# Attention, spectral mixing and w_ch on one core: attention ahead of the weights, x times w_ch in chunks 18 to 27, three gathers

## The chip, the cores and the metric

The kernel runs on one core of one Trainium2 chip. The core has five engines that run their own instruction queues: TensorE (PE, with its weight loads shown apart as PEld), VectorE (DVE), ScalarE (ACT), GpSimd (POOL) and SyncE (SP). POOL and SP also issue DMA transfers, which 16 DMA engines carry. The metric is device microseconds of one execution, the median of several runs; lower is better.

## What is computed

Two stages, the first feeding the second. The sizes are batch 8, heads 8, sequence 576, head width 64, model width 512 and 64 modes; all inputs and the output are float32.

```python
scores = q @ k.T / 8;  cum = cumsum(max(s, 0))
scores = where(causal, -1e9, scores + min(-(cum[:, None] - cum[None, :]), 0))
x = softmax(scores) @ v                       # [8, 576, 512] once heads are merged
X = rfft(x, axis=1)[:, :64]                   # Xr, Xi
Yr = einsum('bmd,mde->bme', Xr, w_r) - einsum('bmd,mde->bme', Xi, w_i)
Yi = einsum('bmd,mde->bme', Xr, w_i) + einsum('bmd,mde->bme', Xi, w_r)
u = x + irfft(Y padded with zeros, n=576, axis=1)
out = u + max(u @ w_ch, 0)
```

`w_r` and `w_i` are 64 matrices of 512 x 512 each, 134 MB of float32 together. Each is read once, and the DMA turns it into bf16 on the way.

## The kernel before

**Attention** (`for n in range(N)`, L583 and after). There are N = 32 iterations; iteration n is head pair g = n // 8 (128 of the 512 columns of x) and batch b = n % 8. In each, `transposes` (L348) turns q and k of the next iteration, `scores` (L382) makes 576 scores a row in two passes and ACT takes the exponential (L406, and L377 for the last 64 keys, once an iteration), `av` (L416) multiplies by v and divides into `x_all`, and `fft` (L450) takes the 64 modes of the iteration before into `xs`. There are two `xs` tiles, used by g % 2; one is cleared by a DVE memset at n = 0, the other at n = 2 (L587).

**Modes** (`modes`, L471). For each g there are eight chunks of eight modes. Chunks are counted through, 0 to 31: chunk c of group g is 8 g + c. A chunk takes two units of weights, w_r and w_i (1 MB of bf16 each, two transfers of 512 KB; the last unit in four of 256 KB), and makes 16 products of 32 columns. For g = 0 to 2 the results gather in `y_acc`; with g = 3 added they are y of that chunk. `mode_steps` (L250) says in which iteration each chunk is computed: chunks 0 to 23 within the attention, one an iteration or so from iteration 9 on, chunks 24 to 31 after it.

**Loads.** All loads of weights, q, k and v stand in one queue, POOL's, in an order written out in the program (`load`, L241). At the head of iteration n come q and k for n + 3 and n + 4 (for odd n), v for n + 3, and weights up to `on_chip[n]`. The weights go to four units inside `x_all` and `y_acc` that are not yet needed, then in turn to the rings `wpool` (5 units) and `wpool2` (3 units, given up from unit 38 on); a transfer waits until the unit that had its place has been used. `on_chip` (L256 to L271) comes from a plan that counts half units and is cut back where the rings are full; in whole units it is

```python
[3, 4, 5, 6, 7, 8, 9, 10, 12, 13, 15, 16, 18, 19, 21, 22, 24, 26, 28, 30, 32, 34, 36, 38, 40, 41, 43, 45, 45, 47, 49, 51]
```

**x times w_ch** is computed apart from y times w_ch, for 18 pairs of row blocks (`pairs`, L519). For 16 of them (`kept`) the product z is copied by ACT into a place in SBUF (`keep_product`, L536) and added later. Six (`first_pairs`) are done in the last six iterations of the attention (`first_transposed`, `first_product`); the others by `work()` (L737), which turns the rows of a pair (`x_transposed`, L656) and keeps the pair before (`keep`, L681). `TAKE` says how many calls follow each chunk of the last group.

**The last group.** y of each chunk is turned (`y_transposed`, L693). For chunks 0 to 3 of the group `gather_round` (L713) brings y and v = y times w_ch together into `yv`, where the rows of all modes stand below each other, 64 rows at once. For chunks 4 and 5 y is gathered so too, but v is computed by `y_times_wch` (L701) and goes to `yv` by a DMA of 128 KB on SP (`spread`, L512). Chunks 6 and 7 are spread both ways. While weights of chunk 6 are awaited, PE computes z of the last kept pair, and between the products of chunk 7 the z sums of pairs 0 and 1 (`first_z`) and the u of pair 0 (`first_u`).

**The end** is a list of steps (L961 and after) that sums, takes the maximum and writes out the 18 pairs, by PE, ACT, DVE, POOL and SP. A DMA of two elements (`mark`, L884) on SP, ahead of the spreads of chunk 6, waits for the last weights.

Of the kernel before, what the change touches and what calls it, by code (L numbers as in the profile page):

```python
# [10 lines left out]
FP32 = mybir.dt.float32  # L11
FP16 = mybir.dt.float16
BF16 = mybir.dt.bfloat16
# [6 lines left out]
def kernel(  # L20
# [11 lines left out]
    nc = tc.nc  # L32
    B, H, S, D = q.shape
    NM = moe_w_r.shape[0]
    DM = H * D
# [68 lines left out]

    xs = [gp.tile([P, 2, 2, 2, 2, B, HM], BF16, name=f"xs{i}") for i in range(2)]
    xs_flat = [t.rearrange("p q k h r b m -> p (q k h r b m)") for t in xs]
# [103 lines left out]
    def ring_of(k):  # L210
        if k < NE:
            return None
        return int(k < LW2 and (k - NE) % (WA + WB) >= WA)
# [35 lines left out]
    NW = 2  # L249
    mode_steps = {B: [0, 1, 2, 3], B + 1: [4], B + 2: [5], B + 4: [6], B + 6: [7]}  # L250
    for c in range(NCK, (NG - 1) * NCK):
        mode_steps.setdefault(B + c - (0 < c % NCK < 4), []).append(c)
    used = [NW * sum(len(cs) for t, cs in mode_steps.items() if t < n) for n in range(N + 1)]
    W0 = 2
    on_chip = []
    for n in range(N):  # L256
        w = 4 + 2 * (WA + WB + NE - 2) * (n + 1) // (B + 1) if n < B else plan + (3 if n <= 2 * B else 4)
        plan = w

        nt, ring = 0, ([], [])  # L260
        while nt < min(w // 2, len(wq)):
            i = ring_of(nt)
            if i is not None:
                depth = (WA, WB)[i]
                if len(ring[i]) >= depth and ring[i][-depth] >= used[n]:
                    break
                ring[i].append(nt)
            nt += 1
        if nt < w // 2:
            plan = 2 * nt + 1  # L270
        on_chip.append(2 * nt)  # L271

# [178 lines left out]
    def fft(n):  # L451
        if n < 0:
            return
        g, b = divmod(n, B)
        ps = auxpool.tile([P, 2, 3 * HM], FP32, name="ft_ps", tag="aux")
        for T in range(NT):
            nT = tails[T]
            for q_ in range(2):
                nc.tensor.matmul(  # L459
                    ps[HP * q_ : HP * q_ + HP].rearrange("p h f -> p (h f)"),  # L460
                    x_all[:nT, g, b, T, q_::2], Ff_sb[:nT, T, :],
                    start=(T == 0), stop=(T == NT - 1),
                    tile_position=(0, HP * q_), skip_group_check=True,
                )
        for h in range(2):
            for q_ in range(2):
                a = ps[HP * q_ : HP * q_ + HP, h, : 2 * HM].rearrange("p (r m) -> p r m", r=2)
                a = bass.AP(tensor=a.tensor, offset=a.offset, ap=[a.ap[0], [HM, 2]] + list(a.ap[1:]))
                nc.vector.tensor_copy(out=xs[g % 2][HP * h : HP * h + HP, q_, :, h, :, b, :], in_=a)  # L469

    def modes(g, c, meanwhile=None):  # L471


        ps = auxpool.tile([P, DM], FP32, name="yp", tag="aux")
        cols = xs[g % 2].rearrange("p q k h r b m -> p q k (h r b) m")

# [50 lines left out]

    first_pairs = [i for i in kept[1:] if pairs[i][0][1] < NF and pairs[i][0][0] <= 4][:6]
    z1s, xts1 = {}, {}

    def kept_place(i, t):

        z1s[i] = t.bitcast(FP32).rearrange("p (x e) -> p x e", x=2)

    def keep_product(i, xx, z):
        nc.scalar.copy(out=z1s[i][:, xx], in_=z)  # L536

    def first_transposed(i, x):
        b, T = pairs[i][x]
        ps = auxpool.tile([P, DT, P], FP32, name="xt_ps", tag="aux")  # L540
        for dt in range(DT):
            nc.tensor.matmul(
                ps[:, dt, :], x_all[:, dt, b, T, :], ident16h, start=True, stop=True,
                skip_group_check=True,
            )
        xts1[i, x] = spool.tile([P, DT, P], FP16, name="xt1", tag="yt")
        nc.vector.tensor_copy(out=xts1[i, x], in_=ps)

    open_unit = {}

    def half_of(pool, name):
# [6 lines left out]
        return t[:, :HU]  # L558

    def first_product(i, x):  # L560
        if x == 0:
            kept_place(i, half_of(wpool2, "z1"))
        ps = auxpool.tile([P, DM], FP32, name="z1_ps", tag="aux")
        for dt in range(DT):
            nc.tensor.matmul(  # L565
                ps, xts1[i, x][:, dt, :], wch_sb[:, dt, :], start=(dt == 0), stop=(dt == DT - 1)
            )
        keep_product(i, x, ps)


# [5 lines left out]
    with tc.tile_pool(name="sc_psum", bufs=2, space=PSUM) as scpool, \  # L576
# [8 lines left out]
        for n in range(N):  # L585
            if n in (0, 2):
                nc.vector.memset(xs_flat[n // 2].bitcast(FP32), 0.0)  # L587
# [18 lines left out]
            scores(n, 1)  # L606
            i = first_pairs[n - N + len(first_pairs)] if n >= N - len(first_pairs) else None
            if i is not None:
                first_transposed(i, 0)
            transposes(n + 1, 1)  # L610
            fft(n - 1)
            av(n, 0)
            if i is not None:
                first_product(i, 0)
                first_transposed(i, 1)
            if i is not None:
                first_product(i, 1)
        av(N - 1, 1)
# [17 lines left out]

    NLOC = 5
    old = xs_flat[0]
    xt_sb = [
# [4 lines left out]

    places = [finpool.tile([P, 4 * DM], BF16, name="r_sb", tag="r", bufs=3) for i in range(2)]
    places += [finpool.tile([P, 4 * DM], BF16, name=f"z1_{i}") for i in range(NLOC)]
    places.append(old[:, 4 * DM : 8 * DM])
    places += [y_acc[:, c : c + 2, :].rearrange("p c e -> p (c e)").bitcast(BF16) for c in (0, 2)]
# [31 lines left out]

    def keep(i):  # L681
        x_times_wch(i, True)
        j = late.index(i)
        kept_place(i, places[j])
        for x in range(2):
            keep_product(i, x, zs.pop((i, x)))
# [25 lines left out]

    def gather_round(c0, c1, b0, which, pool):  # L713

        n = 2 * MC * (c1 - c0)
        ng = P // n
        ps = pool.tile([P, DM], FP32, name="g_ps", tag="u" if pool is upool else "aux")
        for dt in range(DT):
            op = yt_first[:, dt, c0 % NY : c0 % NY + c1 - c0].rearrange("p c (x b) -> p (c x) b", b=B)
            for g in range(ng):  # L720
                nc.tensor.matmul(
                    ps[n * g : n * g + n, :] if which else ps[n * g : n * g + n, bass.ts(dt, P)],
                    op[:, :, b0 + g],
                    wch_sb[:, dt, :] if which else ident16h,
                    start=(dt == 0 or not which), stop=(dt == DT - 1 or not which),
                    tile_position=(0, n * g), skip_group_check=True,
                )

        def copies(engine=None):
            copy = {"v": nc.vector.tensor_copy, "s": nc.scalar.copy}[engine or ("s" if which else "v")]  # L730
            for g in range(ng):
                copy(out=yv[2 * MC * c0 : 2 * MC * c1, b0 + g, which, :], in_=ps[n * g : n * g + n, :])

        return copies

# [13 lines left out]

    late = [i for i in kept if i not in first_pairs]  # L750
    order_z = late[:-1]
    TAKE = (3, 2, 3, 0, 0, 0)
    us, rs = {}, {}
# [89 lines left out]
    def z_of(i):  # L843
        return [zs[i, x] for x in range(2)]

    for c in range(NCK - 2):
        yb = modes(NG - 1, c)
        for x in range(TAKE[c] - 1):
            work()
        if c == NCK - 3:  # L850
            x_transposed(late[-1])
            x_transposed(0)
        yt = y_transposed(yb, c)
        if TAKE[c]:
            work()
        if c >= NY:
            if c == NCK - 3:
                x_times_wch(0, False)
                x_transposed(1)
            y_times_wch(c, yt)  # L860
            if c == NCK - 3:
                for x in range(2):
                    gather_round(NY, NCK - 2, 4 * x, 0, upool)("sv"[x])
        elif c == NY - 1:
            for x, pool in enumerate((auxpool, upool, auxpool, auxpool)):
                for which in (1, 0):
                    gather_round(0, NY, 2 * x, which, pool)()
                if x >= 2:
                    work()
    assert not order_z and not ahead  # L870
    c = NCK - 2
    yb6 = modes(NG - 1, c, {2: lambda: keep(late[-1])})
    x_times_wch(1, False, (0,))
    yt = y_transposed(yb6)
    x_times_wch(1, False, (1,))
    vb6 = y_times_wch(c, yt)


# [11 lines left out]
    def first_z(i):  # L890
        add_y(z_of(i), i, 1, slice(0, GK))
        add_last(z_of(i), i, vb6, c=0)

    yb = modes(NG - 1, NCK - 1, {2: lambda: (first_z(0), first_z(1)), 3: first_u})

# [90 lines left out]
```

## Time and profile before

| what | us |
|---|---|
| median of 3 runs (438.44 to 439.22) | 439.2 |
| the profiled execution, its own time | 440.17 |
| its span, first to last instruction | 438.4 |
| PE busy | 339.6 (77%) |
| DVE busy | 251.8 (57%) |
| ACT busy | 227.6 (52%) |
| POOL busy | 172.5 (39%) |

The span is what the rows of the trace cover; the profiled execution took 1.8 us more than that. The loads through POOL's queue are 81.3 MB as written, the transfers of SP's queue 11.1 MB, of which the output is 9.4. Times in rows of the trace are microseconds from the first instruction. In a row such as `393.23 0.67 PE L479 MATMUL yp<-w_sb,xs ... x8 [1.32 <-DMA w_sb]` stand the start, the length, the engine, the line of the program, the operation with what it writes and reads, how many instructions were drawn together, and in brackets how long the engine had been idle and what ended that. A table by stretch gives for each engine the busy time and, in brackets, the number of instructions, then the granted clock of TensorE (1.00 is full), the mean busy share of the 16 DMA engines (it may pass 1, as packets overlap) and what they wrote in GB/s. The attention's last exponential of a 64-key block starts at 325.16 us, chunk 31's last products at 404.90 us, and the last output is issued at about 435 us.

### The profile page before, as it was taken

Reading aid. Unit: us, or ns where it says so; the run is one execution under the profiler, and the core shown is the slowest. Engines: PE = TensorE matmul, PEld = TensorE weight load, DVE = VectorE, ACT = ScalarE, POOL = GpSimd, SP = SyncE. Lnnn points to the kernel's source line nnn. Section 1 sums busy time; section 2 is a strip of 40 time slices with the busy share of each in tenths; the row PEclk is TensorE's granted clock in tenths of the full one; section 3 lists DMA queues with packets and bytes.
Section 4 is the critical chain, followed back from the end, with each engine's and each line's share of the span. In section 5 each row is a group of like instructions: output and inputs, shape, how many; then the busy total and the mean of one; then the engine's idle time right before and its main releaser. Section 6 shows DMA issues by size and latency. Waiting matters only on the chain. (4 is left out here: it accounts for less than half of the span.)

```text
span 438.4 us, 10539 instructions
## 1 busy us (share of the span) xinstructions
PE 339.6 (77%) x4362; PEld 204.0 (47%) x4409; DVE 251.8 (57%) x572; ACT 227.6 (52%) x424; POOL 172.5 (39%) x258
## 2 busy tenths in 40 slices
PE   1687989899695967973938447888887977778995
PEld 1455666466463544651615224655653535332441
DVE  7667776577564545662624415666655444370796
ACT  1487788268463625760726124666660434330795
POOL 6556354434354444323443433333322221310493
PEclk9999999899987969995877858999997998998999
DMA  9999999999999999999999999999999999996598
GB/s 167 207 207 205 206 206 207 207 209 208 207 205 207 209 207 210 208 209 209 204 209 208 210 208 209 207 210 206 212 211 212 211 211 212 211 216 122 186 380 340
DMA packets 68409, 93.09 MB, mean 212 GB/s; under 512 B 25278, under 2 KB 27066, under 8 KB 68362
## 3 DMA queue, kind: packets, MB, share of 16 engines
q0 software_dynamic: 61424, 81.28, 105.0%
q1 hardware_dynamic: 6938, 11.14, 7.0%
q8 instruction: 34, 0.56, 0.5%
q14 instruction: 13, 0.11, 0.1%
HBM read 163.37 MB, written 9.51 MB: 394 GB/s over the span
## 5 line engine op out<-in xcount | busy, mean ns | idle before, releaser
L406 ACT ACTIVATE p_sb<-sc_ps,cumt_sb 128x576 f16<-128x576 f32 (+1 forms) x256 | 141.7, 636 | 21.8 <-PE sc_ps L398 21.4
L245 POOL DMA_DIRECT2D v<-in_v_dram x72 | 51.3, 713 | 62.1 <-DMA w_sb<-in_moe_w_i_dram 13.5
L398 PE MATMUL sc_ps<-qt,kt 128*128 128x320 bf16 (+2 forms) x337 | 65.6, 299 | 11.3 <-ACT kt L360 6.5
L245 POOL DMA_DIRECT2D w_sb<-in_moe_w_i_dram x62 | 38.4, 620 | 89.2 <-PE yp L479 29.3
L360 DVE COPY qt<-tr_ps 64x576 bf16<-64x576 bf16 x64 | 47.8, 746 | 39.9 <-PE tr_ps L356 39.9
L479 PE MATMUL yp<-w_sb,xs 128*32 128x512 bf16 (+1 forms) x480 | 43.3, 439 | 30.1 <-DMA w_sb<-in_moe_w_i_dram 26.7
L356 PE MATMUL tr_ps<-ident,qk 64*64 64x64 bf16 x1152 | 34.9, 206 | 30.9 <-DMA qk<-in_k_dram 14.6
L245 POOL DMA_DIRECT2D w_sb<-in_moe_w_r_dram x60 | 37.3, 622 | 54.0 <-DMA w_sb<-in_moe_w_r_dram 33.3
L398 PEld LDWEIGHTS <-kt 128*128 128x128 bf16 x384 | 38.4, 105 | 36.1 <-ACT kt L360 14.1
L392 PE MATMUL sc_ps<-negm,ident 128*128 128x256 bf16 x256 | 54.0, 296 | 0.0
L356 PEld LDWEIGHTS <-qk 64*64 64x64 bf16 x1152 | 26.9, 119 | 48.9 <-DVE kt L360 18.9
L377 ACT ACTIVATE p<-sc_ps,cumt 128x64 f16<-128x64 f32 x32 | 10.0, 313 | 74.0 <-PE sc_ps L373 74.0
L434 PE MATMUL av_ps<-v,p_sb 128*128 128x65 f16 x1024 | 44.1, 197 | 1.8 <-DVE x_all L444 0.7
L360 ACT COPY kt<-tr_ps 64x576 bf16<-64x576 bf16 x32 | 22.8, 714 | 40.6 <-DVE qt L360 40.0
L434 PEld LDWEIGHTS <-p_sb 128*128 128x128 f16 x1024 | 37.5, 99 | 9.4 <-DVE x_all L444 5.5
L469 DVE CAST xs<-ft_ps 64x128 bf16<-64x128 f32 x128 | 36.7, 287 | 7.0 <-PE ft_ps L459 5.6
L479 PEld LDWEIGHTS <-xs 128*32 128x32 bf16 (+1 forms) x512 | 17.5, 146 | 48.2 <-DMA w_sb<-in_moe_w_i_dram 26.4
L439 DVE TENSOR_REDUCE den<-av_ps 128x5 f32<-128x10 f32 x64 | 10.9, 170 | 49.7 <-PE av_ps L434 48.8
L444 DVE TENSOR_TENSOR x_all<-av_ps,rcp 128x320 f16<-128x320 f32 x64 | 31.5, 492 | 2.2
L499 DVE TENSOR_TENSOR y_acc<-yp,y_acc 128x512 f32<-128x512 f32 x16 | 11.1, 692 | 28.9 <-PE yp L479 28.2
L459 PE MATMUL ft_ps<-Ff_sb,x_all 128*64 128x192 f16 (+1 forms) x320 | 24.2, 264 | 1.0 <-DVE x_all L444 1.0
L536 ACT COPY z<-z_ps 128x512 f32<-128x512 f32 x22 | 12.9, 585 | 22.8 <-PE z_ps L565 14.2
(112 smaller groups left out, 444.8 us busy)
## 6 DMA issues: line engine op xcount, KB each, us to landing
w_sb<-in_moe_w_r_dram POOLq DMA_DIRECT2D x60, 512.0 KB, 13.5
w_sb<-in_moe_w_i_dram POOLq DMA_DIRECT2D x55, 512.0 KB, 13.2
out_dram<-r_w SPq DMA_DIRECT2D x16, 512.0 KB
v<-in_v_dram POOLq DMA_DIRECT2D x72, 64.0 KB, 11.2
qk<-in_q_dram POOLq DMA_DIRECT2D x15, 288.0 KB, 12.0
qk<-in_k_dram POOLq DMA_DIRECT2D x15, 288.0 KB, 13.2
x_all<-in_moe_w_r_dram POOLq DMA_DIRECT2D x4, 512.0 KB, 9.0
w_sb<-in_moe_w_i_dram POOLq DMA_DIRECT2D x3, 384.0 KB, 12.7
```

What stands on the lines that cost most here:

```text
L245: nc.gpsimd.dma_start(out=dst, in_=src)
L356: nc.tensor.transpose(ps[rows, r, :], src[rows, r, :], ident16[rows, rows])
L360: copy(out=to[:, :, :, half * RH : half * RH + RH], in_=ps[HP * i : HP * i + HP].rearrange("d r (h p) -> d h p r", h=2),)
L392: nc.tensor.matmul(ps[:, bass.ds(w * S, W)], ident16, negm[:, bass.ts(r, W)], start=True, stop=False, skip_group_check=True,)
L398: nc.tensor.matmul(ps[:, c0 : c0 + i1 - i0], keys[:, w, r, :], qh[:, i0:i1], start=False, stop=True, skip_group_check=True,)
L406: nc.scalar.activation(out=pt[:, poff[x] : poff[x] + S - w * W], in_=ps[:, w * S : (w + 1) * S - w * W], func=ACTF.Exp, bias=cumt_sb[:, x, ...
L434: nc.tensor.matmul(ps[:, I, r : r + NCH], lhsT, rhs, start=(i == 0), stop=(i == len(todo) - 1), skip_group_check=True,)
L444: nc.vector.tensor_tensor(out=x_all[:, g, b, :, D * h : D * h + D], in0=ps[:, :, 1 : NCH], in1=rcp.unsqueeze(2).to_broadcast([P, NT, D]), ...
L459: nc.tensor.matmul(ps[HP * q_ : HP * q_ + HP].rearrange("p h f -> p (h f)"), x_all[:nT, g, b, T, q_::2], Ff_sb[:nT, T, :], start=(T == 0), ...
L469: nc.vector.tensor_copy(out=xs[g % 2][HP * h : HP * h + HP, q_, :, h, :, b, :], in_=a)
L479: nc.tensor.matmul(ps[32 * cg : 32 * cg + 32, :], cols[k0:, q_, 1 - ri, :, c * MC // 2 + cg], wt[(g, c, ri)][cg // 2][k0:, 2 * (cg % 2) + ...
L536: nc.scalar.copy(out=z1s[i][:, xx], in_=z)
```

## The change

Five edits that belong together. The order of weights is written as a formula, one unit per iteration and another every eight, and 15 chunks are left to the time after the attention: `mode_steps` now holds chunks 0 to 16. Since chunks 17 to 23 of group 2 then run while group 3's modes are being written, there is a third `xs`, cleared at n = 4. The products x times w_ch leave the attention: `first_pairs`, `first_transposed` and `first_product` go, and `work()` is called after chunks 18 to 27 by a new `TAKE`; the places of the kept products change with that. `gather` replaces `gather_round`: y and v of chunks 0 and 1, 2 and 3, 4 and 5 of the last group are gathered, 32 rows each time, so v of chunks 4 and 5 no longer goes by DMA. In chunk 6, z of the last kept pair and of pairs 0 and 1 moves behind the products, and `first_z(0)` ahead of chunk 7's.

```diff
-    xs = [... for i in range(2)]
+    xs = [... for i in range(3)]
+    XS = (0, 1, 2, 0)
...
-    mode_steps = {B: [0, 1, 2, 3], B + 1: [4], B + 2: [5], B + 4: [6], B + 6: [7]}
-    for c in range(NCK, (NG - 1) * NCK):
-        mode_steps.setdefault(B + c - (0 < c % NCK < 4), []).append(c)
+    mode_steps = {
+        B: [0, 1, 2, 3], 9: [4], 10: [5], 12: [6], 14: [7], 16: [8], 18: [9], 19: [10], 21: [11], 23: [12],
+        25: [13], 26: [14], 28: [15], 30: [16],
+    }
+    done = [c for t in sorted(mode_steps) for c in mode_steps[t]]
...
     for n in range(N):
-        w = 4 + 2 * (WA + WB + NE - 2) * (n + 1) // (B + 1) if n < B else plan + (3 if n <= 2 * B else 4)
...
-        on_chip.append(2 * nt)
+        w = 3 + n if n < B else 4 + n + (n - B) // B
...
+        on_chip.append(2 * w)
...
-            if n in (0, 2):
+            if n in (0, 2, 4):
                 nc.vector.memset(xs_flat[n // 2].bitcast(FP32), 0.0)
...
-            i = first_pairs[n - N + len(first_pairs)] if n >= N - len(first_pairs) else None
-            if i is not None:
-                first_transposed(i, 0)
             transposes(n + 1, 1)
             fft(n - 1)
             av(n, 0)
-            if i is not None:
-                first_product(i, 0)
-                first_transposed(i, 1)
-            if i is not None:
-                first_product(i, 1)
...
-    NLOC = 5
-    old = xs_flat[0]
+    NLOC = 3
+    old = xs_flat[1]
...
+    places = [lambda: half_of(wpool2, "z1")] * (2 * WB)
+    places.append(old[:, 4 * DM : 8 * DM])
...
+    places += [xs_flat[2][:, i * 4 * DM : (i + 1) * 4 * DM] for i in range(2)]
...
+    def gather(c0, c1, turns, kinds, then=None):
+        n = 2 * MC * (c1 - c0)
+        rows = slice(2 * MC * c0, 2 * MC * c1)
+        ng = P // n
+        for b0 in range(0, B, ng):
+            for which in kinds:
+                pool, tag = then if then and b0 else (auxpool, "aux")
+                ps = pool.tile([P, DM], FP32, name="g_ps", tag=tag)
+                for dt in range(DT):
+                    for g in range(ng):
+                        op = yt_first[:, dt, c0 % NY : c0 % NY + c1 - c0].rearrange("p c (x b) -> p (c x) b", b=B)
+                        nc.tensor.matmul(
...
+                            tile_position=(0, n * g), skip_group_check=True,
+                        )
+                for g in range(ng):
+                    dst, src = yv[rows, b0 + g, which, :], ps[n * g : n * g + n, :]
+                    if (which == 0 and (b0 == 0 or g < 2)) if then else g % 2:
+                        nc.vector.tensor_copy(out=dst, in_=src)
+                    else:
+                        nc.scalar.copy(out=dst, in_=src)
...
-    late = [i for i in kept if i not in first_pairs]
+    late = list(kept)
...
-    TAKE = (3, 2, 3, 0, 0, 0)
+    TAKE = {18: 2, 19: 2, 20: 2, 21: 2, 22: 2, 23: 2, 24: 1, 25: 1, 26: 1, 27: 1}
...
+    for c in range(len(done), (NG - 1) * NCK):
+        modes(c // NCK, c % NCK)
+        for x in range(TAKE.get(c, 0)):
+            work()
     for c in range(NCK - 2):
         yb = modes(NG - 1, c)
-        for x in range(TAKE[c] - 1):
-            work()
         if c == NCK - 3:
             x_transposed(late[-1])
             x_transposed(0)
         yt = y_transposed(yb, c)
-        if TAKE[c]:
+        for x in range(TAKE.get((NG - 1) * NCK + c, 0)):
             work()
-        if c >= NY:
-            if c == NCK - 3:
-                x_times_wch(0, False)
-                x_transposed(1)
-            y_times_wch(c, yt)
-            if c == NCK - 3:
-                for x in range(2):
-                    gather_round(NY, NCK - 2, 4 * x, 0, upool)("sv"[x])
...
+        if c == NCK - 3:
+            x_transposed(1)
+        if c % 2:
+            gather(c - 1, c + 1, (), (1, 0), (upool, "u"))
...
-    yb6 = modes(NG - 1, c, {2: lambda: keep(late[-1])})
-    x_times_wch(1, False, (0,))
+    yb6 = modes(NG - 1, c)
+    keep(late[-1], (0,))
     yt = y_transposed(yb6)
-    x_times_wch(1, False, (1,))
+    keep(late[-1], (1,))
     vb6 = y_times_wch(c, yt)
+    x_times_wch(0, False)
+    x_times_wch(1, False)
...
-    yb = modes(NG - 1, NCK - 1, {2: lambda: (first_z(0), first_z(1)), 3: first_u})
+    first_z(0)
+    yb = modes(NG - 1, NCK - 1, {2: lambda: first_z(1), 3: first_u})
```

## The prediction

> **What bounds the kernel now.** I read first the forty slices of the page, then the sums by stretch, then who waits for whom, then the rows in order of time. In the slices, three rows matter: TensorE's clock, the share of the DMA engines and the bytes they write.
>
> ```profile
> PE   1687989899695967973938447888887977778995
> PEclk9999999899987969995877858999997998998999
> DMA  9999999999999999999999999999999999996598
> GB/s 167 207 207 205 206 206 207 207 209 208 207 205 207 209 207 210 208 209 209 204 209 208 210 208 209 207 210 206 212 211 212 211 211 212 211 216 122 186 380 340
> ```
>
> The DMA row stands at 9 from the first slice to the thirty-sixth, about 395 us, while PE drops to 1, 3 and 4 tenths on the way. So the stream of loads is the bound up to about 404 us. By stretch (busy time of PE, PEld, DVE, ACT, POOL; then granted clock, DMA share, GB/s):
>
> ```profile
> 22.00:77.00 55.00, 48.25 (x793) 32.86 (x798) 39.91 (x106) 43.33 (x82) 28.15 (x44) 1.00 1.21 206
> 77.00:264.00 187.00, 137.22 (x1988) 85.89 (x2016) 95.67 (x234) 88.80 (x165) 74.39 (x115) 0.83 1.18 208
> 330.00:398.00 68.00, 54.36 (x486) 28.69 (x484) 32.85 (x55) 22.95 (x40) 14.59 (x24) 0.92 1.12 212
> 414.00:437.00 23.00, 19.36 (x90) 7.72 (x87) 18.92 (x18) 19.55 (x39) 16.45 (x14) 1.00 0.99 384
> ```
>
> The share is above 1.1 in every stretch of loading, and the rate moves only with the mix: 206 GB/s where one weight unit comes per iteration, 212 where there are weights alone. After 409 us the end is a chain of sums with ACT full and the output written at 384 GB/s. The waits say the same:
>
> ```profile
> ACT p L377 <- PE sc_ps L373: 74.0, 31, 11.6
> POOL w_sb L245 <- DMA w_sb<-in_moe_w_r_dram: 47.1, 28, 3.1
> POOL w_sb L245 <- DMA w_sb<-in_moe_w_i_dram: 31.2, 24, 2.0
> POOL w_sb L245 <- PE yp L479: 30.4, 7, 7.0
> ```
>
> POOL, which issues all loads, is held mostly by earlier loads that have not landed. The attention (ACT's 74 us at L377) pays for it, at no cost to the end. Last, the stretch in which the last two chunks of weights land:
>
> ```profile
> 393.23 0.67 PE L479 MATMUL yp<-w_sb,xs 128*32 128x512 bf16 x8 [1.32 <-DMA w_sb<-in_moe_w_i_dram]
> ...
> 398.73 0.67 PE L479 MATMUL yp<-w_sb,xs 128*32 128x512 bf16 x8 [1.91 <-DMA w_sb<-in_moe_w_r_dram]
> 399.33 0.12 PEld L764 LDWEIGHTS <-G_sb 96*128 96x128 f16 x2 [0.38 <-issue]
> ...
> 402.92 0.65 PE L479 MATMUL yp<-w_sb,xs 128*32 128x512 bf16 x4
> ...
> 403.62 0.26 SPq L884 DMA_DIRECT2D mark<-w_sb  x1
> ...
> 404.90 0.65 PE L479 MATMUL yp<-w_sb,xs 128*32 128x512 bf16 x4
> ```
>
> SP's mark at 403.62 waits for the last weights alone, so they land at 403.6. The last products start at 404.90, 1.3 us later: from 399.3 on PE, not the load, sets the end, because the sums of z for pairs 0 and 1 (399.33 to 402.92) ran at half clock:
>
> ```profile
> 395.98:399.39 3.41, 1.50 (x13) 0.51 (x12) 0.69 (x1) 0.00 (x0) 0.00 (x0) 1.00 0.97 181
> 399.39:402.80 3.41, 3.41 (x14) 0.90 (x12) 0.00 (x0) 0.00 (x0) 0.00 (x0) 0.50 0.53 99
> ```
>
> PE was busy 1.50 of 3.41 us in the first of these stretches, and in the next the granted clock is 0.50.
>
> **The change, part by part.** *Order of the loads.* The bytes stay the same; units of weights move behind the attention. Through iteration 9 both plans give 3, 4, 5 and so on to 10, 12, 13 units. Then the old plan adds one and a half to two units per iteration, the new one a single unit and an extra one every eight. What this costs hangs on whether the DMA engines ever run dry. Two iterations then load 2 units (2.10 MB) and attention data (two tiles of 288 KB, four of 64 KB: 0.85 MB); 2.95 MB at 206 GB/s are 14.3 us, 7.2 each, and the extra unit (1.05 MB at 212, 4.95 us) over eight iterations makes 7.8. PE needs 6.6 us for an iteration that waits for nothing (L373 at 96.71 and 103.13 are 6.4 apart; L377 at 60.83 and 67.56 are 6.7 apart) and 1.09 us for a chunk (L479, sixteen products). Thirteen chunks in iterations 9 to 31 add 0.6: 7.2 us. So the loads stay slower than PE by about half a microsecond an iteration, and POOL starts iteration 9 with loads that take 12 to 14 us from issue to landing queued ahead. I take 0 us; the attention ends near 262 us instead of 330 (73.7 us, 16 for iteration 8, 22 of 7.8). The bound on the other side is the third rival's: 3.5 us.
>
> *Third xs and its clearing.* One more DVE memset of 1.76 us (L587) at iteration 4. At iteration 2 the same memset made that iteration 7.7 us instead of 6.6, so 1.1 us of PE, covered by the queue of loads (9 to 11 us to landing there). 0 us; 1.1 if that queue were empty.
>
> *Products x times w_ch.* The six pairs done in the last six iterations go (L542 4.6, L565 12.4 us of PE; iterations of 9.3 and 10.4 us there) and come back among chunks 18 to 27. One call costs PE 0.62 + 1.9 us, DVE 1.4, ACT 1.2; two per chunk are 5 us, with the chunk 6.1, under 9.9 us for a chunk's two units at 212 GB/s. Even all at half clock, 12 us now and then is covered by three units in flight, 14.8 us. 0 us.
>
> *Three gathers.* Each makes 2 rounds of v (16 products, 1.1 us each) and y (16, 0.36), then 16 copies, 10 on ACT (0.58) and 6 on DVE (0.69). Those of chunks 1 and 3 of the last group lie in 9.9 us of load each: 0. For the one of chunk 5, ACT has 5.8 us of copies from about 387.3, done near 393.1, a hair before chunk six's copies need ACT (394). I charge 0.4 us, since chunk 5 now starts from an idle PE, thus at half clock; bounds 0 and 1.3.
>
> *Two spreads of v less.* The SP transfers of v for chunks 4 and 5 go: 128 KB each, at 212 GB/s 0.62 us of the stream each. The first comes before chunk six's last weights, the second before chunk seven's: chunk six lands 0.6 earlier, the end of weights 1.2. Bounds: 0 (if the engines had room) and 1.0 for chunk six, by nothing better than that load rates at 384 to 388 us show 220 against 212 GB/s in sum.
>
> *The path from chunk six to the last product of chunk seven.* Before: 393.23 to 405.55, 12.3 us, with 1.9 idle and about 1.7 lost to the clock. After, at full clock: products 0.6; keep's first half 0.87; ACT copies z and then yt, 0.59 and 0.58, so v starts at 2.95 (the transposes and keep's second half, 0.40 and 0.87, lie inside); v 0.87; sums of pairs 0 and 1 that were done in earlier waits, 16 matmuls of 0.216, 3.46; first z of pair 0 four of them, 0.86; products 0.5; z of pair 1 half of 1.79, 0.9; products 0.5; first u 1.40 (403.50 to 404.90); products 0.65. Sum 12.1. So 3.8 us of PE work moved behind chunk six is paid by the filled 1.9 us and by the clock. What is queued behind the moved z on ACT is yt alone, and v waits for it; that is in the sum.
>
> *The end.* From 405.55 on nothing changes: 32.9 us of span.
>
> **Sum.** 0.6 earlier landing, 0.2 shorter path, 0.4 later ACT: 0.4 to 0.5 us less. The profiled execution took 440.2 us, 1.8 around its span of 438.4, so it would take 439.7; it stands 1.0 above the median 439.2, which becomes 438.7 us.
>
> **Rivals.** *Clean path:* ACT is done in time and the spread's whole effect is felt: 0.2 + 1.0, 438.0 us. For: DVE and ACT sums above; against: PE idles before chunk five. The Trainium skill, "TensorE: Matmul & The Clock Gate", section "HAM oscillation — how this bites in real kernels", asks for no PE gaps over about 3.4 us; by that rule the waits of about 2 us around chunk six cost no clock and this case stands, while here a gap of 1.9 us was enough, so I do not follow it.
>
> *The clock falls inside the path.* The gather of chunk 5 ends on PE near 389, its next work is 0.6 us, and chunk six lands near 392.5. A stretch like 395.98 to 399.39 then falls before the path and the next 3.41 us run at half clock: up to 1.7 us, 1.3 where ACT's copies are waited for anyway. 0.5 less and 1.3 to 1.7 more: 440.0 us at most, 439.9 taken.
>
> *The loads run dry* (the other side). POOL issues q of iteration n+3 only when PE has transposed iteration n. The queue of some 10 us lasts 22 iterations if PE takes 0.45 us more than the loads, so it decides from 7.8 + 0.45 = 8.25 us an iteration; what PE takes beyond that is lost to the stream for good. At 8.4 us it is 22 times 0.15, some 3.5 us with the start of an empty queue: 442.7. For: mean clock 0.83 from 77 to 264 us, and each half-clock stretch costs 1.7 us. Against: these lie behind waits that now go; from 22 to 77 us the clock is 1.00.
>
> *It does not do what it says:* loads still lead, attention waits as before, 439.2.
>
> **How the numbers follow.** A measurement tells about 0.2% here, 0.9 us. Forecast 0.36 (0.13 faster by more than that, 0.20 within, 0.03 slower), clean path 0.22 (0.20 and 0.02), clock 0.16 (0.09 within, 0.07 slower), dry 0.19 (slower), no effect 0.07 (within). Faster 0.33, same 0.38, slower 0.29. The range, 437.2 to 442.0, leaves out about 0.04 below and 0.11 above; the forecast's own is 438.0 to 439.4.
>
> **What would show it.** Right: the last L373 near 258 us; DMA row at 9 until the same slice; no yv<-v_sb spread before the mark; the mark near 402.4; last products of chunk seven near 405.0 and the same 33 us after. Wrong: a slice under 9 between 90 and 262 us with POOL waiting for PE tr_ps (dry); clock 0.50 between 392 and 404 (clock); a copy of yt over 0.5 us late behind L732 copies on ACT (gather); a tail longer than 33 us would be something I have not priced.

## The result, and the profile after

The changed kernel is slower by half a per cent: 441.7 us median of 11 runs (440.58 to 442.78) against 439.2 of 11 runs of the kernel before on the same chip; the ratio is 1.0047, 95% interval 1.0031 to 1.0063, so about 2.1 us more by the ratio, where 438.7 us was forecast. Its profiled execution took 441.87 us with a span of 440.1; before it was 440.17 with 438.4. The two traces can be compared for the 1.7 us between their spans. They do not stand alike in their runs: the execution of before is 1.0 us above its median, the one of after 0.2.

The slices of the page after, the rows that were read before:

```profile
PE   1598889899999799699699995577776758289995
PEclk9998999999999799999699999888888686679999
DMA  9999999999999999999999999999999999995498
GB/s 166 207 206 206 204 207 207 208 208 207 204 206 208 207 208 210 199 206 209 208 208 208 195 212 211 212 211 211 211 211 211 211 211 211 211 211 109 167 382 335
```

The DMA row stays at 9 to the same slice, so the loads do not run dry for long. But PE's weak slices have moved: it is mostly at 8 and 9 to slice 24, and in the twelve after it at 5 to 8 but for one at 2; the clock is .6 to .8 in slices 26 to 36, up to the end of the loads. In the row of rates two slices stand out, 199 GB/s from 176 to 187 us and 195 from 242 to 253. The same stretches as before (busy time of PE, PEld, DVE, ACT, POOL; clock, DMA share, GB/s):

```profile
22.00:77.00 55.00, 48.72 (x792) 33.21 (x790) 39.95 (x100) 41.92 (x79) 28.54 (x44) 0.97 1.21 206
77.00:264.00 187.00, 166.02 (x2646) 107.56 (x2645) 125.98 (x317) 123.17 (x232) 81.02 (x126) 0.95 1.19 206
330.00:398.00 68.00, 43.55 (x441) 21.84 (x440) 24.81 (x37) 27.96 (x49) 14.56 (x24) 0.75 1.12 211
414.00:437.00 23.00, 20.90 (x97) 8.41 (x94) 20.30 (x19) 21.09 (x42) 17.71 (x15) 1.00 0.93 361
```

From 77 to 264 us PE now works 166 instead of 137 us, at clock 0.95 instead of 0.83, and the stream writes 206 instead of 208 GB/s: the attention runs ahead. Its last L371 (L377 before) starts at 263.9 instead of 325.2 us. From 330 to 398 us the clock is 0.75. The waits:

```profile
POOL w_sb L246 <- DMA w_sb<-in_moe_w_i_dram: 54.2, 33, 2.6
POOL w_sb L246 <- DMA w_sb<-in_moe_w_r_dram: 49.1, 31, 2.2
...
ACT p L371 <- PE sc_ps L367: 35.6, 30, 5.6
...
POOL w_sb L246 <- PE yp L473: 17.6, 6, 5.3
```

ACT's wait for scores, 74.0 us before, is halved. That is off the path. What sets the end is the stretch from chunk six on, in order of time (start, length, engine, line):

```profile
390.57 5.87 ACT L703 CAST yv<-g_ps 32x512 f16<-32x512 f32 x10 [2.01 <-PE g_ps L691]
...
390.80 4.19 DVE L701 CAST yv<-g_ps 32x512 f16<-32x512 f32 x6 [1.05 <-PE g_ps L691]
...
392.95 1.22 PE L473 MATMUL yp<-w_sb,xs 128*32 128x512 bf16 x16 [1.09 <-ACT yv L703]
...
395.02 0.69 DVE L497 TENSOR_TENSOR y_sb<-yp,y_acc 128x512 f16<-128x512 f32 x1
...
395.77 0.40 PE L662 MATMUL yt_ps<-ident16h,y_sb 128*128 128x128 f16 x4 [0.62 <-DVE y_sb L497]
...
396.46 0.59 ACT L529 COPY y_acc<-z_ps 128x512 f32<-128x512 f32 x1
396.95 0.59 ACT L664 COPY yt_sb<-yt_ps 128x512 f16<-128x512 f16 x1
...
397.59 1.04 PE L670 MATMUL v_ps<-wch_sb,yt_sb 128*128 128x512 f16 x4 [0.57 <-ACT yt_sb L664]
...
398.47 1.89 PE L641 MATMUL z_ps<-wch_sb,xs 128*128 128x512 f16 x8
...
400.19 1.89 PE L641 MATMUL z_ps<-wch_sb,xt_x 128*128 128x512 f16 x8
...
402.88 0.67 PE L473 MATMUL yp<-w_sb,xs 128*32 128x512 bf16 x8
...
403.51 0.26 SPq L851 DMA_DIRECT2D mark<-w_sb  x1
...
406.44 0.65 PE L473 MATMUL yp<-w_sb,xs 128*32 128x512 bf16 x4
```

The same rows of the kernel before:

```profile
393.95 0.69 DVE L503 TENSOR_TENSOR y_sb<-yp,y_acc 128x512 f16<-128x512 f32 x1 [1.42 <-PE yp L479]
...
395.14 0.58 ACT L698 COPY yt_sb<-yt_ps 128x512 f16<-128x512 f16 x1 [2.28 <-PE yt_ps L696]
```

Four things are to be seen. The copies of the gather keep DVE to 394.99 and ACT to 396.44, so y of chunk six is summed at 395.02 (before 393.95) and turned y copied at 396.95 (before 395.14). PE waits twice for them, 0.62 and 0.57 us. Only behind v come the sixteen products of z for pairs 0 and 1 (398.47 to 402.1), which nothing had held back. And chunk seven's first products start at 402.88, although their weights landed at 398.48. The last products end at 407.09, 1.54 us later than before, and the end after them takes 33.0 us of span as before (32.85).

In the records of the loads, each with one execution (us from the span's start; "last" is the last quarter of chunk seven; the last column is the time from the issue of the last output to the end of the span):

| kernel | chunk 5 landed | chunk 6 | last | last products end | behind the last issue |
|---|---|---|---|---|---|
| before | 382.24 | 393.19 | 403.60 | 405.55 | 3.06 |
| after | 383.76 | 393.48 | 403.50 | 407.09 | 3.19 |
| a_both_old | 383.51 | 393.63 | 405.27 | 407.11 | 3.72 |
| b_new_tail | 382.29 | 392.90 | 402.80 | 405.82 | 5.00 |
| c_gather_old | 382.92 | 393.22 | 403.61 | 406.83 | 3.74 |
| d_z_old | 383.75 | 393.69 | 403.64 | 407.40 | 3.20 |
| f_z0_first | 382.15 | 393.81 | 404.22 | 404.92 | 3.06 |
| h_old_tail_z0 | 383.49 | 393.68 | 404.04 | 404.73 | 3.74 |
| c_warm | 383.69 | 394.00 | 404.43 | 407.24 | 4.07 |
| g_unit_early | 383.08 | 393.02 | 403.01 | 406.61 | 3.19 |
| i_fill | 382.76 | 392.71 | 403.31 | 404.79 | 3.19 |
| m_fill_unit | 382.90 | 392.84 | 403.72 | 405.02 | 3.18 |
| k_spread_off | 382.36 | 393.34 | 403.38 | 406.62 | 4.47 |
| l_spread_thrice | 383.05 | 394.29 | 405.50 | 415.12 | 3.35 |

From chunk six's landing to the end of the last products, which is called the path below, it is 12.36 us before and 13.61 after: 1.25 of the 1.7 us. The rest is 0.29 of landing and 0.1 of the end. The last column will matter below: from the issue of the last output on no engine computes, and yet it is not the same in all kernels. The traces of a_both_old, c_gather_old and d_z_old are 2.2, 1.0 and 1.3 us above the medians of their kernels, so single rows of these say little of the usual execution.

### The profile page after: what moved, and what is told of

Its sections match the earlier page's. It is cut to its first block, busy times and chain, and to the rows that moved or that the text cites. A ratio compares the mean times of both kernels' runs of the same rounds, so it can differ in the third digit from the quotient of the medians.

```text
span 440.1 us, 10802 instructions
## 1 busy us (share of the span) xinstructions
PE 349.0 (79%) x4497; PEld 205.6 (47%) x4497; DVE 255.9 (58%) x577; ACT 237.9 (54%) x442; POOL 172.4 (39%) x258
## 3 DMA queue, kind: packets, MB, share of 16 engines
q1 hardware_dynamic: 6650, 10.88, 6.8%
## 5 line engine op out<-in xcount | busy, mean ns | idle before, releaser
L392 PE MATMUL sc_ps<-qt,kt 128*128 128x512 bf16 (+2 forms) x384 | 75.4, 308 | 6.7 <-ACT kt L354 5.5
L473 PE MATMUL yp<-w_sb,xs 128*32 128x512 bf16 (+1 forms) x480 | 41.8, 425 | 36.9 <-DMA w_sb<-in_moe_w_i_dram 31.1
L392 PEld LDWEIGHTS <-kt 128*128 128x128 bf16 x384 | 37.0, 103 | 35.1 <-ACT kt L354 14.5
L386 PE MATMUL sc_ps<-negm,ident 128*128 128x256 bf16 x256 | 53.0, 291 | 0.2
L350 PE MATMUL tr_ps<-ident,qk 64*64 64x64 bf16 x1152 | 31.9, 200 | 21.6 <-DVE kt L354 19.3
L350 PEld LDWEIGHTS <-qk 64*64 64x64 bf16 x1152 | 24.6, 113 | 35.2 <-DVE kt L354 25.8
L529 ACT COPY z<-z_ps 128x512 f32<-128x512 f32 x18 | 10.5, 585 | 46.0 <-PE z_ps L641 33.8
L641 PE MATMUL z_ps<-wch_sb,xs 128*128 128x512 f16 x96 | 30.7, 476 | 0.0
L371 ACT ACTIVATE p<-sc_ps,cumt 128x64 f16<-128x64 f32 x32 | 10.0, 313 | 35.6 <-PE sc_ps L367 35.6
```

The source lines that it names most:

```text
L350: nc.tensor.transpose(ps[rows, r, :], src[rows, r, :], ident16[rows, rows])
L386: nc.tensor.matmul(ps[:, bass.ds(w * S, W)], ident16, negm[:, bass.ts(r, W)], start=True, stop=False, skip_group_check=True,)
L392: nc.tensor.matmul(ps[:, c0 : c0 + i1 - i0], keys[:, w, r, :], qh[:, i0:i1], start=False, stop=True, skip_group_check=True,)
L473: nc.tensor.matmul(ps[32 * cg : 32 * cg + 32, :], cols[k0:, q_, 1 - ri, :, c * MC // 2 + cg], wt[(g, c, ri)][cg // 2][k0:, 2 * (cg % 2) + ...
L641: nc.tensor.matmul(zs[i, x], xts[i][:, x, dt, :], wch_sb[:, dt, :], start=(dt == 0), stop=(last and dt == DT - 1), skip_group_check=True,)
```

## The experiments

Ratios are to runs of the kernel before on the same chip (medians there 439.6 us, 21 to 25 runs).

**Which part costs: one back at a time.** Four kernels: `a_both_old` is the changed kernel with both late parts (gather of chunks four and five, places of z) as before, so its order of loads, with the third xs, the products x times w_ch and the gathers of chunks one and three in their new form; `c_gather_old` has the old gather, `d_z_old` the old places of z; `b_new_tail` is the kernel before with both new late parts.

```diff
 # a_both_old and c_gather_old, against after: chunks 4 and 5 (gather_round is put back)
-        if c % 2:
-            gather(c - 1, c + 1, (), (1, 0), (upool, "u"))
+        if c >= NY:
+            ...
+            y_times_wch(c, yt)
+            if c == NCK - 3:
+                for x in range(2):
+                    gather_round(NY, NCK - 2, 4 * x, 0, upool)("sv"[x])
+        elif c % 2:
+            gather(c - 1, c + 1, (), (1, 0), (upool, "u"))
 # a_both_old and d_z_old, against after: z of pair 0 in chunk 5, then chunks 6 and 7
         if c == NCK - 3:
+            x_times_wch(0, False)
             x_transposed(1)
...
-    yb6 = modes(NG - 1, c)
-    keep(late[-1], (0,))
+    yb6 = modes(NG - 1, c, {2: lambda: keep(late[-1])})
+    x_times_wch(1, False, (0,))
     yt = y_transposed(yb6)
-    keep(late[-1], (1,))
+    x_times_wch(1, False, (1,))
     vb6 = y_times_wch(c, yt)
-    x_times_wch(0, False)
-    x_times_wch(1, False)
...
-    first_z(0)
-    yb = modes(NG - 1, NCK - 1, {2: lambda: first_z(1), 3: first_u})
+    yb = modes(NG - 1, NCK - 1, {2: lambda: (first_z(0), first_z(1)), 3: first_u})
```

> The changed kernel's attention, order of weights and products among chunks 18 to 27, but chunks 4 to 7 of the last group as before: gather of 4 and 5 with v by DMA, and z of pairs 17, 0 and 1 in their old places. Theory (the loss of 2 us is made in those last chunks): last products of chunk seven near 405.5 us, time at the kernel before's, within 0.5 us. Rival (the new order of loads loses time in the stream): weights land 0.6 us or more later than 403.6, time 0.6 to 2 us above before.

> The changed kernel, with chunks 4 and 5 gathered as before (y alone on PE, v by DMA), z of pairs 17, 0 and 1 in the new places. Theory of the gather (its 10 copies on ACT and 6 on DVE hold up y and yt of chunk six by about 1.2 us): 1.0 to 1.5 us below the changed kernel. Rival (the 16 moved matmuls alone lengthen PE's path): less than 0.4 us below it.

> The changed kernel with its three gathers, but z of pairs 17, 0 and 1 and the first z in their old places. Theory of the gather: yt of chunk six still late, and the old half-clock stretch may come back: within 0.7 us of the changed kernel. Rival (the moved matmuls): 1.3 us or more below it, at before's time.

> The kernel before with chunks 4 to 7 of the last group in their new form (gather of 4 and 5 with v on PE, z behind chunk six, first z of pair 0 ahead of chunk seven), all else as before. Theory (last chunks): 1.5 to 2.5 us above before, as in the changed kernel; yt of chunk six copied over a microsecond later than 395.14 because copies of yv are ahead of it. Rival (order of loads): at before's time or up to 1 us below, since two DMA transfers of v go.

| kernel | median us | ratio | interval |
|---|---|---|---|
| a_both_old | 440.34 | 1.0019 | 1.0006 to 1.0032 |
| c_gather_old | 441.25 | 1.0046 | 1.0027 to 1.0065 |
| d_z_old | 440.80 | 1.0027 | 1.0016 to 1.0039 |
| b_new_tail | 442.71 | 1.0072 | 1.0057 to 1.0086 |

a_both_old is 0.8 us above before, and I had put all that is new in it at nothing. But this is not yet a price of the order of loads: in its trace 0.7 us more than before (3.72 against 3.06) lie behind the issue of the last output, where no weights are awaited. The new places of z cost 0.9 to 1.2 us (after against d, c against a; in both pairs the ends behind the last issue are alike, but the intervals overlap a little). The new gather costs nothing that can be told beside the new places of z (after against c) and 0.4 us without them (d against a; the intervals overlap); in both pairs the kernel with the old gather ends about 0.5 us longer behind the last issue, so equal times do not show that the gather is free. That the path of c gains nothing has a reason in its trace, three stretches around the landing of its chunk six at 393.22:

```profile
389.00:393.00 4.00, 1.84 (x42) 0.85 (x41) 3.15 (x5) 2.30 (x4) 0.17 (x1) 0.93 1.12 211
393.00:396.40 3.40, 3.13 (x17) 1.23 (x17) 0.99 (x2) 0.20 (x1) 0.00 (x0) 0.51 1.12 223
396.40:400.00 3.60, 3.60 (x19) 1.53 (x18) 0.69 (x1) 1.46 (x3) 0.00 (x0) 1.00 1.08 203
```

The row of PE that starts that path:

```profile
393.26 1.08 PE L473 MATMUL yp<-w_sb,xs 128*32 128x512 bf16 x8 [2.43 <-DMA w_sb<-in_moe_w_i_dram]
```

Without the new gather's products PE is busy for 1.84 of 4 us and waits 2.43 us for the landing, and the clock falls to 0.51 in the path itself: turned y is copied 3.46 us after the landing, as in after (3.47). So in that execution the rival in which the clock falls happened, in this kernel though not in after. Of b_new_tail's 3.1 us, 1.9 lie behind the last issue (see k_spread_off); its turned y is copied at 395.67, 0.5 us later than before, where the theory had over a microsecond.

**The short path before, the order of loads again, PE kept busy, one unit earlier.** `f_z0_first` puts the first z sum of pair 0 ahead of chunk seven and changes nothing else; `h_old_tail_z0` does the same to a_both_old. `c_warm` is c_gather_old with ten products more in the wait of chunk six, into a place that is then started anew. `g_unit_early` is after with one unit more in the plan from iteration 26 on.

```diff
 # f_z0_first, against before
-    yb = modes(NG - 1, NCK - 1, {2: lambda: (first_z(0), first_z(1)), 3: first_u})
+    first_z(0)
+    yb = modes(NG - 1, NCK - 1, {2: lambda: first_z(1), 3: first_u})
 # c_warm, against c_gather_old
-    yb6 = modes(NG - 1, c)
+    yb6 = modes(NG - 1, c, {2: busy})
 # g_unit_early, against after
         w = 3 + n if n < B else 4 + n + (n - B) // B
+        w += n >= 26
```

> The kernel before with one edit: the z sums of pair 0 stand ahead of chunk seven's products and not between them. Theory (from chunk six on the end is set by PE, and the half-clock stretch from 399.4 us comes from the idle 1.9 us before it): the idle time is filled, no half clock there, last products at 404.3 us behind the last weights at 403.6 and not at 405.55; 1.0 to 1.4 us below before. Rival (the end hangs on the weights alone): within 0.4 us of before.

> The changed kernel's attention and order of loads with the old last chunks (as in a_both_old) and that same single edit. Theory: 0.5 to 1.4 us below a_both_old, so about at before's time; above f_z0_first by what the order of loads costs, 0.5 to 1.0 us. Rival (the order of loads costs nothing, a_both_old was 0.8 above by chance): equal to f_z0_first within 0.4 us.

> c_gather_old with ten idle matmuls in the wait for chunk six's last weights, into a bank of z that is overwritten by the next product; nothing else. Theory (without the gather PE idles, the clock falls to 0.50 at 393 us and takes back what the gather's absence gives): the clock stays at 1.00 from 392 to 404, last products about 12.3 us after chunk six's landing and not 13.6; 0.8 to 1.4 us below c_gather_old. Rival (the moved matmuls themselves are the 1.2 us): within 0.4 us of c_gather_old.

> The changed kernel with one unit of weights more from iteration 26 on. Theory (the rate falls to 146 to 185 GB/s at 246 to 249 us because few bytes are in flight behind small loads of v): the dip goes or shrinks, weights land 0.4 to 0.7 us earlier, 0.3 to 0.7 us below the changed kernel. Rival (the dip costs nothing, or is not of the order): no difference over 0.3 us.

f_z0_first: 439.31 us, 0.9998 (0.9985 to 1.0011); the gain that was expected of it is not there, though its trace has no half clock in the path and its last products start with the landing:

```profile
404.24 0.25 SPq L884 DMA_DIRECT2D mark<-w_sb  x1
...
404.27 0.65 PE L479 MATMUL yp<-w_sb,xs 128*32 128x512 bf16 x4 [0.39 <-DMA w_sb<-in_moe_w_i_dram]
```

There its end is set by the loads, so a shorter path can give no more. That the kernel before loses time to the path in its profiled execution (1.3 us behind the landing) and yet gains nothing here suggests that this execution, 1.0 us above the median, is not the usual one. h_old_tail_z0: 440.25 us, 1.0014 (1.0005 to 1.0023), 0.9 us above f_z0_first on the same chip, as was expected. Yet its trace does not show the cause that was expected: its weights land 0.2 us earlier than those of f_z0_first and its last products end 0.2 us earlier, and again 0.7 us (3.74 against 3.06) lie behind the last issue. c_warm: 442.43 us, 1.0051 (1.0037 to 1.0065), by the ratios 0.2 us above c_gather_old: the gain that the theory expected is not there. The clock was at 1.00 from 393.0 us on, through the whole path. But the ten products, from 392.40 on, held chunk six's last products to 394.93, 0.9 us behind the landing (0.04 in c_gather_old). The path is 13.24 us against 13.61, so most of what the clock gives is taken back by the delay; what a clock kept up without delay would give is not shown. g_unit_early: 441.35 us, 1.0037 (1.0025 to 1.0050), 0.4 us under after, with intervals that overlap. In its slice from 242 us the rate is 204 GB/s and not 195, but i_fill, without the unit, has 202 there.

**Same instructions, other order in chunk six; and the spreads.** `i_fill` is after with five lines reordered: z of pair 0 stands before the turning of y, the copy of turned y ahead of the copies of z on ACT. `m_fill_unit` adds g_unit_early's line. `k_spread_off` is f_z0_first with the new gather in place of the two v spreads; `l_spread_thrice` is the kernel before with each of them sent three times.

```diff
 # i_fill, against after
-    keep(late[-1], (0,))
+    x_times_wch(0, False)
     yt = y_transposed(yb6)
-    keep(late[-1], (1,))
+    keep(late[-1])
     vb6 = y_times_wch(c, yt)
-    x_times_wch(0, False)
     x_times_wch(1, False)
 # k_spread_off, against f_z0_first
-            y_times_wch(c, yt)
-            if c == NCK - 3:
-                for x in range(2):
-                    gather_round(NY, NCK - 2, 4 * x, 0, upool)("sv"[x])
+                gather(NY, NCK - 2, (), (1, 0), (upool, "u"))
 # l_spread_thrice, against before
-            spread(c, 1, vb)
+            for _ in range(3):
+                spread(c, 1, vb)
```

> The changed kernel, same instructions, other order on PE and ACT in chunk six: the z sums of pair 0 before the turning of y, the copy of yt on ACT ahead of the two copies of z, both halves of the kept product before v. Theory (the moved sums cost because they stand behind v, while PE waits for yt): PE is busy from 394.2 on without a wait, chunk seven's first products start near 401.5 instead of 402.9, last products near 405.8, 1.3 us less, 440.4 us, ratio 1.0015 to 1.0025. Rival (the work itself is too much for the time there is, or the landing sets the end): 0 to 0.3 us less, 1.0040 to 1.0047.

> The same order, and one unit of weights more in the plan from iteration 26 on, so that the weights land 0.4 us earlier. If path and stream both limit in part: 0.3 to 0.5 us less than i_fill, 440.0 us, ratio 1.0008 to 1.0018. If the path alone sets the end: the same as i_fill.

> The kernel before with the new gather of v for chunks four and five, so the two transfers of v gone, and the first z sum of pair 0 ahead of chunk seven; z of the other pairs in its old places. Theory (the spreads cost the weights 0.3 to 0.8 us, and with the short path the end follows the landing): 0.3 to 0.8 us less than the kernel before, 438.8 to 439.3, ratio 0.9982 to 0.9993. Rival (the gather's copies on ACT make yt of chunk six late and take it all back): 439.6 to 440.3, ratio 1.0000 to 1.0016.

> The kernel before, with the two transfers of v for chunks four and five sent three times each, so 512 KB more on SP's queue. Theory (they take their time from the weights, 0.62 us each): last weights 2 to 2.5 us later, 441.6 us, ratio 1.0045 to 1.0055; so two fewer would give 1.2 us of landing. Rival (the engines have room for them): 439.3, ratio within 1.0010.

i_fill: 439.82 us, 1.0009 (1.0000 to 1.0019), 1.7 us under after by the two ratios: the theory's side, even below its range. Its path, in order of time:

```profile
392.17 1.24 PE L473 MATMUL yp<-w_sb,xs 128*32 128x512 bf16 x16 [1.01 <-ACT yv L703]
...
393.34 1.90 PE L641 MATMUL z_ps<-wch_sb,xs 128*128 128x512 f16 x8
...
394.31 0.69 DVE L497 TENSOR_TENSOR y_sb<-yp,y_acc 128x512 f16<-128x512 f32 x1
...
395.07 0.39 PE L662 MATMUL yt_ps<-ident16h,y_sb 128*128 128x128 f16 x4
...
395.67 0.58 ACT L664 COPY yt_sb<-yt_ps 128x512 f16<-128x512 f16 x1
...
397.02 1.03 PE L670 MATMUL v_ps<-wch_sb,yt_sb 128*128 128x512 f16 x4
...
400.57 0.67 PE L473 MATMUL yp<-w_sb,xs 128*32 128x512 bf16 x8
...
404.14 0.65 PE L473 MATMUL yp<-w_sb,xs 128*32 128x512 bf16 x4
```

y is summed as late behind the landing (392.71) as in after, 1.6 us, and v starts later behind it, 4.3 instead of 4.1 us. But PE waits for neither, since eight more products of z are done ahead of v, and chunk seven's first products start 7.9 us behind the landing instead of 9.4. The path is 12.08 us instead of 13.61. m_fill_unit: 439.72 us, 1.0000 (0.9989 to 1.0011): with both edits the changed kernel is as fast as the one before; whether the unit adds to the order is not told apart (the intervals overlap).

k_spread_off: 443.06 us, 1.0079 (1.0063 to 1.0095), worse than both theories had it. In the trace the gather holds chunk six's first products, with weights that were there at 387.33, to 393.97, and turned y is copied at 399.40, 6.1 us behind the landing:

```profile
393.97 0.67 PE L479 MATMUL yp<-w_sb,xs 128*32 128x512 bf16 x8 [1.09 <-ACT yv L760]
...
397.13 0.69 DVE L503 TENSOR_TENSOR y_sb<-yp,y_acc 128x512 f16<-128x512 f32 x1 [1.13 <-PE yp L479]
...
399.40 0.59 ACT L698 COPY yt_sb<-yt_ps 128x512 f16<-128x512 f16 x1 [0.85 <-PE yt_ps L696]
```

The last products end 1.7 us later than in f_z0_first. Another 1.4 us come behind the issue of the last output: k_spread_off and b_new_tail end 4.5 and 5.0 us after it, f_z0_first and the kernel before 3.1. In the sums by microsecond of k_spread_off (the last two columns are DMA share and GB/s) a remnant trails:

```profile
437.00:438.00 1.00, 0.00 (x0) 0.00 (x0) 0.00 (x0) 0.00 (x0) 0.00 (x0) 0.86 1.06 410
438.00:439.00 1.00, 0.00 (x0) 0.00 (x0) 0.00 (x0) 0.00 (x0) 0.00 (x0) 0.50 0.14 49
439.00:440.00 1.00, 0.00 (x0) 0.00 (x0) 0.00 (x0) 0.00 (x0) 0.00 (x0) 0.50 0.03 12
```

From 438.3 to 439.3 us the share is 0.06 at 25 GB/s, as much as one of the sixteen engines makes. The ends fall into groups: 3.1 us with the old order and the old gather (3.35 in l_spread_thrice), 3.2 with the new of both, 3.7 to 4.1 with the new order and the old gather (a_both_old, c_gather_old, h_old_tail_z0, c_warm), 4.5 and 5.0 with the old order and the new gather. Why is open; each is one execution.

l_spread_thrice: 450.36 us, 1.0252 (1.0233 to 1.0270), far beyond what was expected, and not for the reason that was tested. Sent to the same rows, each transfer waits for the one ahead, so SP's queue is held for 26 us, 22.2 of them waiting for transfers of the same kind, and the first z sum waits for it:

```profile
380.38 25.97 SPq L514 DMA_DIRECT2D yv<-v_sb  x6
```

```profile
408.88 1.01 PE L765 MATMUL z_ps<-yv,G_sb 96*128 96x512 f16 x2 [8.94 <-DMA yv<-v_sb]
```

Its time is therefore no measure. Its last weights landed at 405.50 instead of 403.60: four transfers more, 0.48 us each, in one execution; against the 404.22 of f_z0_first it is 0.32.

## Why the prediction was wrong

**Order of the loads, 0 us: not refuted, and not confirmed.** I argued that PE stays ahead of the loads by half a microsecond an iteration and that they thus never run dry. PE stayed ahead (the last 22 iterations, from 91.81 to 263.88 us by L371, took 7.8 us each, as summed, not the third rival's 8.25; the attention ended at 264 us, 262 were forecast), but the stream loses some time at first. Chunk five lands at 382.15 to 382.36 us in the four traces with the old order and unchanged or fewer spreads, and at 382.8 to 383.8 in the nine with the new one, a mean of 383.3: 1.1 us. At chunk six little is left of it: with the spreads it lands at 393.19 and 393.81 under the old order and at 393.22 to 394.00 under the new, without them at 392.90 and 393.34 against 392.71 to 393.69; the means differ by 0.1 us and less. By the runs it is 0.8 to 0.9 us (a_both_old; h_old_tail_z0 against f_z0_first), but 0.7 of these lie behind the last issue by the traces, and the 0.1 to 0.3 that are left are less than the intervals can tell from nothing. Part of the place of the early loss is seen. After, and then before:

```profile
240.00:260.00 20.00, 18.81 (x314) 12.03 (x311) 14.29 (x35) 13.99 (x28) 7.63 (x13) 1.00 1.15 202
```

```profile
240.00:260.00 20.00, 11.44 (x134) 5.97 (x132) 6.43 (x15) 5.30 (x10) 7.14 (x11) 0.73 1.16 209
```

202 instead of 209 GB/s for 20 us is 0.7 us; between two halves of a weight unit, at 241.9 to 245.9, POOL issues nothing for 4.0 us there. In the twenty-third slice of the page (from 242 us in after) all nine traces with the new order have 194 to 204 GB/s and the five with the old 209 or 210, and in the seventeenth (from 176 us) it is 198 to 203 against 207 to 209. But attention data pass in the stretch from 240 us after and not before, i_fill shows 206, and no run isolates this gap.

**Third xs, products x times w_ch, gathers of chunks one and three, 0 us:** none was tried alone. They stand in a_both_old too, so what they cost is within its 0.8 us, and they may have a part in its longer end.

**Two spreads less, 0.6 us each: right in kind, too large.** From chunk five's landing to chunk six's it is 10.12 to 10.31 us with the spread and 9.72 to 9.95 without, under the new order: 0.3 us. From there to the last weights the medians are 10.41 and 10.02: 0.4, but the values spread (10.36 to 11.64, and 9.95 to 10.88). So of the 0.6 us at chunk six about half came. That chunk six landed 0.29 us later in after than in before, and not 0.6 earlier, is within the scatter: the other four kernels without spreads and with the new order have it at 392.71 to 393.69.

**Gather of chunk five, 0.4 us of the bounds 0 to 1.3: mis-sized.** I had ACT's copies done near 393.1, and DVE's I did not follow. The sign that I had named for it came, a copy of yt late behind ACT's other copies. Chunk five landed 1.5 us later, then three turns of x and the first products of the gather ran at half clock; the copies began at 390.57 and not at 387.3, and ended at 396.44. v started 4.11 us behind the landing, not 2.95: 1.2 us in place of 0.4, near the upper bound. The 2.95 itself is not fully accounted for, as the terms named for it make 2.64. The old gather instead (c_gather_old) makes the path no shorter, since the clock falls there.

**The path of 12.1 us: the step that failed most.** It took 13.61 us. The lengths in it were nearly right: from v to the last products it took 9.50 us where 9.15 were summed. What failed is that the work moved behind chunk six should be paid in part by "the filled 1.9 us". In after it filled nothing: PE stood still for 0.62 and 0.57 us ahead of v while 3.46 us of z, which needed nothing of chunk six, stood behind v in its queue. i_fill has the same instructions and the same late copies, with eight of these products ahead of v; its path is 12.08 us. That this is also the sum that I had made is luck: I had v at 2.95 and 9.15 from there, i_fill has 4.31 and 7.77. The runs show what the order is worth: 1.7 of the 2.1 us are undone by order alone, with intervals that lie apart. i_fill changes the order on PE and on ACT together; as v starts no earlier in it, the gain is seen on PE.

**Half clock gone from the path, about 1.7 us:** it did go (1.00 from 395 us on in after), but the profiled execution of before, whose clock loss I counted as a gain to come, seems not to have been the usual case (f_z0_first). I also took the 1.0 us by which that execution stood above its median off the forecast; the one of after stood only 0.2 above its own, so 0.8 us of the miss come from there. **The end, 32.9 us:** 33.0 measured.

Of the rivals, none came about in after as it was told. The dry loads had the right sign (442.7), but by another mechanism: neither did iterations take 8.25 us, nor did the order of loads make most of the loss. The rival in which the clock falls was added up too low: 0.5 less and 1.7 more is 440.4 us, not 440.0 at most. The clock's fall inside the path is seen in c_gather_old, at the end of a wait of PE of 2.43 us. The Trainium skill, "TensorE: Matmul & The Clock Gate", section "HAM oscillation — how this bites in real kernels", asks for no idle gap over about 3.4 us; the trace does not agree, a shorter gap was enough, as in the kernel before.

## What to carry to other kernels

When work moves to where the last loads are awaited, do not only add its lengths: write the queue of each engine in order, and put what is ready ahead of what must wait for another engine. A gather that replaces a transfer takes copies on two engines, and these must be free when the next chunk's results come; here they were not, and once PE had other work ahead, what that cost was no longer clear of the noise. A single profiled execution that stands 1 us above its median may hold a loss that the usual one does not have: do not count its removal as a gain without a second look. And before a difference between two kernels is put down to the part that was edited, see where in the trace it lies: here 0.7 us that looked like a price of the loads lay behind the issue of the last output.

## What was not expected of the hardware

A 128 KB transfer on SP's queue beside a stream of 210 GB/s delayed the weights by 0.3 to 0.5 us and not by the 0.6 of its bytes, in few executions that scatter by as much. With the same output issued in the same steps, the last bytes trailed for 1.4 to 1.9 us more in two kernels, at 49 GB/s and less, and for 0.7 to 1.0 us more in four others, in one of them (h_old_tail_z0, 436.3 to 436.9 us) at 24 GB/s; no run shows why.
